# Attention and a gated feed-forward block in one kernel: the late loads and some stores issued by ScalarE's queue, the plan of the order made anew

## The chip, the core and the metric

The kernel runs on one core of one Trainium2 chip. The core has five engines, each with an instruction queue of its own that is worked off in order: TensorE (PE in the profile, with its weight loads as PEld), VectorE (DVE), ScalarE (ACT), GpSimd (POOL) and SyncE (SP). SyncE computes nothing; it issues DMAs. ScalarE can issue DMAs too, and then the issue is one more instruction in the queue that its arithmetic goes through. The metric is the device time of one execution in microseconds, lower is better. Before the change the median of six runs was 271.02 us (270.65 to 273.36).

## The reference, cut to what matters

```python
def _attn_ref(q, k, v, is_retrieval, n_sink, window):     # q, k, v: (4, 8, 768, 64)
    scores = scale * np.matmul(q, k.transpose(0, 1, 3, 2))
    stream_keep = causal & (is_sink | in_win)              # 4 sinks, window of 64
    mask = np.where(retr, full_mask, stream_mask)          # heads 0, 2, 6 see all of the past
    scores = np.where(mask, scores, -1e9)
    a = np.exp(scores - scores.max(-1)); a = a / a.sum(-1)
    return np.matmul(a, v)

def _moe_ref(x, w_gate, w_val, w_out):                     # x: (3072, 512), d_ff = 1536
    g = x @ w_gate
    silu = g * (1.0 / (1.0 + np.exp(-g)))
    return (silu * (x @ w_val)) @ w_out
```

Attention over 4 batches of 8 heads, of which three are causal and five see only 4 sink positions and the last 64; its output, laid out as 3072 tokens of 512, goes through a gated feed-forward block.

## The kernel before, in words

**Tiles.** The 3072 tokens are 24 tiles of 128 queries; two tiles are a pair, and there are 12 pairs, numbered 0 to 11 in the order `QP` (line 142). Six groups of four tiles (`SIZES`, line 149) go through the feed-forward block together. Group 0 is tiles 0 to 3, group 1 tiles 4 to 7, and so on.

**What is done for a pair.** Its q, k and v (called x in the loads) come by one DMA of 512 KB each into a buffer of the ring `raw`, which has 11 buffers (`load`, lines 324 to 340; L330 is q, k and v, L335 and L338 are the weights). The buffers are taken in turn, so that a load can start once the buffer of the load eleven places earlier has been read. Casts (line 185 on DVE and POOL, 183 on ACT) make float16 copies. q and k have to be transposed: for the early pairs by TensorE (`transposes`, L472) with a copy out of PSUM, for the later ones by transposing DMAs (`dmaq` L449 and `dmak` L457, where a `dmak` issues two DMAs). The constants `XQK` and `XK` say from which pair on: 5 for q, 7 for k.

**What is done for a tile.** Scores on TensorE (L594) into PSUM, an exponential on ScalarE (L604, up to 1024 columns at a time), for tiles from 4 on a mask by multiplication on DVE or POOL (L612), the product with v (L624), reciprocal and normalisation (L629, L641). The result `xb` is transposed into `xt`, by TensorE (L657) for tiles below `XBAR` = 8 and by a DMA on SyncE (L651) from there on.

**Feed-forward.** For each group twelve steps j: gate and value products (L875, four matmuls each), tanh on ScalarE (L881), two combinations on DVE (L885, L892); then the output product (L904), copied out of PSUM (`oevac`, on ACT or DVE) and stored by two DMAs of 128 KB (`store`, L928).

**The order.** Every step above is a `Task` with a list of `ways` it can be done (engine and two costs), and the order in which the program is written out is not computed here: it is a string, `ORDER` (line 16). Each two of its digits, in base 62, are a number; below 3700 it is a task, and 3700 + n stands for n matmuls on the identity (`warm`, L305), whose result nobody reads. `WAYS` (line 44) has a digit for each task that picks one of its ways. `Plan.order` (line 102) reads both. So costs, due times and the rings `queue` and `queue2` in the task list leave no trace in the program; what counts is the order of the tasks on each engine and the engine chosen. An engine that reaches a task whose inputs are not there waits, and all that is behind it in its queue waits with it. In the kernel before, all DMAs but one are issued by SyncE: 54 loads, 47 of the 48 halves of stores, and the transposing DMAs (16 for xt, 14 for q, 20 for k).

Of the kernel before, what the change touches and what calls it, by code (L numbers as in the profile page):

```python
# [16 lines left out]
    "000B010A0C0E0D0G0I050F030K2H2I060H04xq07080O2K2J2G0Jy52U090S2L2N2O2Vxv2P2M0L2W022Q0M2z3u2R3t0P2S"  # L17
    "300U322T31yQ2X0T372Y2Z383C0N2a392j0Q1w3D2e2l2k2b3E2m2f0Vxj2n5U2c0c2d1x212p3A2r2o2g2q0R2s3B34330m"
    "xs2u2h3o2v3F3r2t2i0d2w3p0Y2x352y3G0n22xoBM10BWBN1z3H1y3PBO36BX3I0Z3J0o3qBP5VBYBZBQ3K3QBg11Ba28Bq"
    "3L0q3M3sBj3R3b0pBr3T0W3S25Bs3N3U3VBh0r3Oxs3W5R5S0sBi3XxlBt3Y5P5Q23Bu3Z0X3a0u3eBkBR5T3dBb0tBlBSBc"  # L20
    "3c3m0a3f3iBT3hBmBd0vBU240g3n3gBeBn3v3j4dBV3wBoBf0bBv0e3k4PC04cBpBw3l4Q0hC5C1Bx123x4SC2By0fC6C33y"
    "Bz0i27C74X134RC4C80y2B4Y40C90jCA4Z162ACF410z3zCD18CBCG26CC431745444a14CHCK2DCE194B4246CL0kCP4CCM"
    "15CI4b20CQ0w4E2CCR4D0lCeCJ4F1ACU0x2F4H1C29CNCV4I4JCW1BCZ1E4eCO2ECS4GCa4g1D1G4UCTCX4V4WCb4hCf4T4K"
    "1F4i1I4fCYCc47Cd4j1H1K48Cg4k5C4LCh4m4M1J5DCi5ICk4n5E5K1M5J4q5H1L5L4oCl1O4p5G5M4w5FCm4r4xCj1Q4l49"
    "1N6F4zCn4s4y4ACoCq501P5N644t1SCr62675O66521R1UCs53654u6H56Ct4v54Cp1W5557Cw1TCu51614N635Y6q585X1Y"
    "1VCx6s4O6u596v5Z5A6ECy5B1X5W6A6r605b6tD25c7jCzCv6CD3D01ZD75a7PD5D8687R6D7Q5g6B5e5d5h705fD1D4715m"
    "696GD9DC7S7Z5nD6DH7lDD7iDADEDI5o6oDFDJ1a7a6pDB1cDM1bDG7bDKDN7UDPDO1d5iDLDR1eDQ5p7TDS7cDW1g5q1fDT"
    "8VDUDX5j5s8G1i5rDYDb5t1h6yDVDg8H8KDc8U6IDh1jDd5uDZ6JDiDeDa8J6z8I6w6KDl8L8XDqDf6x8Q6L5vDmDjDrDn6M"
    "E0Ds7ODk7kDv966N8R5k976O5wDw8S5l7NDo6PDxDtDp6QDy6RDu1k8T6YDz1mE16Z1l1o5x5y6S8W6a6b6TE26c1n6UE36e"
    "6VE4E66f1p6d6iE76W6j6g5zE86h9h7XE572E96X6k9r737YEC9m6l9k9l7B9jED747C6m9sEE9AA37D7EEA6nEF9i757F76"  # L30
    "EI9tEB98EO9B997HA1EPER7IEQ7V9uET7GESEYEUEG7WA2Am7JEVEZEW7h7K9GEH7fEdEaAn7d8FEXEbEe8EEg7g8O9HEf77"
    "EJEc8M8PEiEh78En8NEjElEk79EoEqEp7L7A95EmEsEr7M1qEx94Et1sEvEy1r1uEu7m9IEzF07nEw1tF2F17oF7F31vFCF8"
    "F47pF9FDEK7q9JFEF5EL7eFMAYEMF67rA0AZFAENAiAc7uAb7sFH7tFBAa80FIAp7vFFAkAj81FJFKAdFG8283FL7w84FN7x"
    "Al7y86858887FO899C7zAo8YFP8A8ZFSFQ9D8B8b8a8CFRFT8c8i9E8DFU8d8j8eFV9FFk8fFWFYFlFX8gFpFm8h9gFuFq9f"
    "FZFrFv8oFwFa8p8kFb8r8qFnFc8sFsFoFd8lFxFt8mFzFyFe8t8nG0G2G1G4G38uG58yFf8v8zG6G78wG8Fg9p8x9KFhG99n"
    "9q9L90GA9MFi9oGC9TGBFjGE9U91AWGJGD92GF9VGOGGGK939WGLGPGiAe9XGQ9ZAXGHAfGM9Y9aAgGIGRGNAh9b9w9xGTGS"
    "9c9zGj9d9NGUGW9O9v9y9eGV9PGY9QGdGXGZ9RGbGaGe9SGfGgGcA4GhH6A5GkH7A6A7GlHBH8A8GmH9HCA9GnGoHAAAGpHD"
    "ABAIACAJGqADHEAKGrHGHFHLHHHJHIGsHMHOHNGtHKHQHPAEHRALAFHVAMHSAGGuHWANAHAOHXHTAPAQHUGvARAqGwArASGx"
    "HaAsGyH0HbATGzAtAUH1AuHcB0AVH2AvB1AwH3HfAxH4HYHgH5AyHdHZAzHhB6B2HeB7HiB3B8HkB4HjB9HlHnB5BAHmBGHp"
    "HoBHBBBCHqI4BDHrHsBEHtI5BFBIHuBJHzBKHvHxHwI0BLI2I1HyISI3IXITIVIUIYIcIZIWIaIdIfIeIbIhIgI6IiIkIjI7"  # L40
    "ImIlI8IrInI9JQIoIsIpItIwIqIuIxIzIyIvJ1J0J6J2JBJ3J7J4J8JCJ9JDJ5JEJAJGJFJLJHJJJIJMJOJNJKJRJPJSJTJW"
    "JUIAJXJVIBJYICJZJcJaIDIGJbIEJdIFIHJeIIJfJiJgIJIMJhIKJjILINJkIOJlJmIPJnIQIR"
)
WAYS = (
    "000010000000000000000000000000000000000000000000000000000000000000000000000000000000000000000000"
    "000000000000000000000000211000010000000010111000010010011000100000000000000000000001000000200010"
    "000000010000000000000000000000011001101000001110110110010000000000100000100000000000000100110000"
    "110000010000000000001001000000000010101001000011001000010010000000000000000000000000100000200000"
    "000100001000000000000000000100000000000010011000000100100000000000000000012000022000000001011010"
    "100010000000000000000000000000100011010000000000110010000000000000001001000000000010001102000000"  # L50
    "000010000000000000000000010110000000000110111001001001000000000010000000000021000210000000001010"
    "001000000000000000000000000000000000000000000000000000000000000000000000000000000000000000000000"
    "000000000000000000000000010000000000010000000000000000000000000000000000000000000000000000000000"
    "000000000000000000010000010000000000000000000000000000000000000000000000000000000000000000000000"
    "000000010000000000000000000000000000000000000000000000000000000000000000000000000000000000000000"
    "000000000000000000000000000000000000000000000000000000000000000000010000000000000000000000000000"
    "0000000000000000000000000000000000000000000000000000000000000000000000000000"
# [55 lines left out]
def kernel(  # L113
# [35 lines left out]
    SIZES = [4, 4, 4, 4, 4, 4]  # L149
# [13 lines left out]
             "h": 2 * NJ, "osb": 2, "gv": 3, "o": 1, "sc": 1, "av": 1, "tr": 1, "queue": 4}  # L163
# [155 lines left out]


# [3 lines left out]
    def load(kind, n):  # L324
        r = buf("raw", [128, 1024], FP, "raw")
        landed[kind, n] = r
        if kind in "qkx":
# [2 lines left out]
            nc.sync.dma_start(  # L330
                out=r.rearrange("p (h x) -> p h x", h=H),
                in_={"q": q, "k": k, "x": v}[kind][b, :, sl, :].rearrange(
                    "h (p j) d -> p h (j d)", j=2))
# [336 lines left out]
    def tasks_of_pair(n):  # L670
# [38 lines left out]
        if xqk:  # L709
            oldq = [x for t in (2 * n - 4, 2 * n - 3) for x in T_sc_of[TILES[t]]]  # L710
            T_dq[n] = [moved(P.add(
                f"dq{n}.{j}", [("SP", 1.27, 1.27, 0)], pos - 0.05,
                (lambda n=n, j=j: dmaq(n, j)), deps=[cs[0, j], T_fill0] + oldq,
                grp=f"pair{n}", takes=["queue", "queue"]), 0.9, 1.1) for j in range(2)]
            T_ev[n, 0] = T_ev[n, 1] = T_dq[n]
        if xk:
            T_ev[n, 2] = [moved(P.add(
                f"dk{n}.{j}", [("SP", 2.5, 2.5, 0)], pos - 0.04,
                (lambda n=n, j=j: dmak(n, j)), deps=[cs[1, j]] + older,
                grp=f"pair{n}", takes=["queue"]), 0.7, 0.7) for j in range(2)]  # L720
# [197 lines left out]

    def store(g, tt):
# [10 lines left out]
    for g in range(NG):  # L930
# [111 lines left out]
```

## Time and profile before

The median is 271.02 us. One execution was profiled; it took 270.79 us, of which 269.0 are the span from its first to its last instruction.

| | |
|---|---|
| median of 6 runs | 271.02 us |
| the profiled execution, its span | 270.79, 269.0 us |
| PE, PEld, DVE busy | 94%, 54%, 61% |
| ACT, POOL busy | 65%, 36% |
| DMA | 42.01 MB, mean 156 GB/s |
| longest chain, by engine | PE 71%, ACT 12%, DMA 7%, SPq 6% |

Busy time of PE counts a matmul until its result is out, and the next one starts long before that, so the start of one to the start of the next is the measure of what a matmul costs. DMA-issuing instructions are not counted as busy time of ScalarE or SyncE; they stand in the order of time with the letter q after the engine's name (SPq, ACTq).

### The profile page before, as it was taken

The numbers are of one execution on the slowest core, as the hardware profiler recorded it, in microseconds if no ns is written. First come the engines' busy times: TensorE is split into PE (matmuls) and PEld (weight loads), VectorE is DVE, ScalarE is ACT, GpSimd is POOL, SyncE is SP. The second block draws the span as 40 slices with busy tenths as digits, with TensorE's granted clock in tenths as the row PEclk, the third lists the DMA queues.
The fourth block names the chain that finished last, engine by engine and source line by source line (L and its number), as shares of the span: only waits on it lengthen the run. The fifth ranks groups of instructions, "written<-read, shape, count | busy, mean of one in ns | idle before, by whom it ended". The sixth has DMA issues, their size and how long they took to land.

```text
span 269.0 us, 5256 instructions
## 1 busy us (share of the span) xinstructions
PE 254.0 (94%) x1971; PEld 146.0 (54%) x1971; DVE 165.0 (61%) x332; ACT 175.9 (65%) x292; POOL 96.8 (36%) x125
## 2 busy tenths in 40 slices
PE   7999789999999999979999899999999999999991
PEld 7877556566655555634446455545555554444440
DVE  7565777688468776458865266677664557775001
ACT  3899998989995996877566654776455643232111
POOL 8748868665293533582065200430021320000000
PEclk9999999999999999999999999999999999999999
DMA  7999999999997977956684811651212200100343
GB/s 192 307 333 331 305 332 379 313 290 288 298 228 187 264 117 200 185 104 140 171 193 75 142 39 22 137 99 23 67 30 62 59 2 20 39 2 0 90 105 78
DMA packets 78520, 42.01 MB, mean 156 GB/s; under 512 B 30880, under 2 KB 73888, under 8 KB 78496
## 3 DMA queue, kind: packets, MB, share of 16 engines
q1 hardware_dynamic: 78416, 41.56, 63.1%
q8 instruction: 15, 0.25, 0.4%
q10 hardware_dynamic: 80, 0.13, 0.2%
q14 instruction: 9, 0.07, 0.1%
HBM read 28.31 MB, written 6.29 MB: 129 GB/s over the span
## 4 chain that ended last, share of the span: by engine, by line
PE 71%; ACT 12%; DMA 7%; SPq 6%; DVE 2%; issue 2%; ACTq 0%
PE gv L875 38%; PE o_ps L904 20%; PE sc L594 7%; PE av L624 4%; DMA raw<-in_v_dram 3%; SPq L330 3%; ACT v L183 3%; ACT e L604 2%; DMA xt<-xb 2%; ACT hq L183 2%; ACT vt L183 2%; ACT sig L881 2%; DMA kT<-hq 1%; SPq L457 1%; DVE sil L885 1%
## 5 line engine op out<-in xcount | busy, mean ns | idle before, releaser
L604 ACT ACTIVATE e<-sc 128x1024 f16<-128x1024 f32 (+4 forms) x71 | 62.3, 881 | 20.6 <-PE sc L594 20.4
L875 PE MATMUL gv<-xt,wg_sb 128*128 128x512 f16 (+1 forms) x304 | 70.3, 368 | 2.9 <-DMA xt<-xb 2.4
L875 PE MATMUL gv<-xt,wv_sb 128*128 128x512 f16 (+1 forms) x304 | 71.0, 368 | 1.1 <-DVE sil L885 1.0
L904 PE MATMUL o_ps<-wo_sb,h 128*128 128x512 f16 x288 | 70.6, 379 | 0.3 <-DVE o_sb L185 0.2
L881 ACT ACTIVATE sig<-gv 128x512 f32<-128x512 f32 (+1 forms) x76 | 43.4, 576 | 41.5 <-PE gv L875 40.4
L885 DVE SCALAR_TENSOR_TENSOR sil<-sig,gv 128x512 f32<-128x512 f32 (+1 forms) x76 | 49.6, 658 | 33.5 <-ACT sig L881 33.0
L612 POOL TENSOR_TENSOR e<-e,m 128x640 f16<-128x640 f16 (+1 forms) x20 | 33.8, 1689 | 60.6 <-ACT e L604 59.0
L892 DVE SCALAR_TENSOR_TENSOR h<-sil,gv 128x512 f16<-128x512 f32 (+1 forms) x76 | 48.6, 655 | 10.3 <-PE gv L875 9.3
L875 PEld LDWEIGHTS <-wg_sb 128*128 128x128 f16 x304 | 28.7, 98 | 30.5 <-issue 2.9
L875 PEld LDWEIGHTS <-wv_sb 128*128 128x128 f16 x304 | 28.9, 98 | 29.9 <-issue 1.9
L904 PEld LDWEIGHTS <-h 128*128 128x128 f16 x288 | 26.9, 98 | 26.0 <-issue 0.7
L594 PE MATMUL sc<-qT,kT 128*128 128x256 f16 (+1 forms) x228 | 35.6, 257 | 1.5 <-ACT e L604 1.5
L594 PEld LDWEIGHTS <-kT 128*128 128x128 f16 x228 | 20.4, 98 | 12.3 <-issue 2.1
L624 PEld LDWEIGHTS <-e 128*128 128x128 f16 x472 | 20.1, 97 | 8.7 <-ACT e L604 1.9
L185 POOL COPY v<-vt 32x528 f16<-32x528 f16 (+1 forms) x34 | 22.1, 651 | 5.6 <-DVE vt L185 4.1
L624 PE MATMUL av<-vt,e 128*128 128x65 f16 x392 | 21.8, 193 | 1.4 <-DVE xb L641 0.8
L185 POOL CAST vt<-raw 64x512 f16<-64x512 f32 x24 | 15.7, 657 | 16.1 <-PE av L624 10.3
L641 DVE TENSOR_TENSOR xb<-av,rc 128x256 f16<-128x256 f32 x47 | 19.9, 424 | 1.6
L183 ACT COPY o_sb<-o_ps 128x512 f32<-128x512 f32 x17 | 9.9, 585 | 14.9 <-PE o_ps L904 13.4
L629 DVE RECIPROCAL rc<-av 128x4 f32<-128x4 f32 x48 | 8.5, 179 | 17.6 <-PE av L624 17.3
L183 ACT COPY v<-vt 2x528 f16<-2x528 f16 (+1 forms) x30 | 18.8, 626 | 0.4
L183 ACT CAST hq<-raw 128x512 f16<-128x512 f32 x27 | 16.2, 617 | 3.7 <-DMA raw<-in_q_dram 2.9
(62 smaller groups left out, 185.5 us busy)
## 6 DMA issues: line engine op xcount, KB each, us to landing
raw<-in_q_dram SPq DMA_DIRECT2D x12, 512.0 KB, 5.3
raw<-in_k_dram SPq DMA_DIRECT2D x12, 512.0 KB, 6.7
raw<-in_v_dram SPq DMA_DIRECT2D x12, 512.0 KB, 6.8
out_dram<-o_sb SPq DMA_DIRECT2D x47, 128.0 KB, 2.4
raw<-in_moe_w_gate_dram SPq DMA_DIRECT2D x6, 512.0 KB, 8.2
raw<-in_moe_w_val_dram SPq DMA_DIRECT2D x6, 512.0 KB, 8.5
raw<-in_moe_w_out_dram SPq DMA_DIRECT2D x6, 512.0 KB, 9.2
kT<-hq SPq DMA_TRANSPOSE x20, 2.4
```

Of the source, the lines that this page charges most:

```text
L183: nc.scalar.copy(out=dst, in_=src)
L185: ENG[task.way[0]].tensor_copy(out=dst, in_=src)
L594: nc.tensor.matmul(sc[c // 4][:, c % 4:c % 4 + n, :], weights, moving, start=first, stop=last)
L604: nc.scalar.activation(out=e[:, 0:n], in_=whole_sc.pop((t, u))[:, 0:n], func=AF.Exp, scale=scale)
L612: ENG[task().way[0]].tensor_tensor(out=ev, in0=ev, in1=mm, op=ALU.mult)
L624: nc.tensor.matmul(av[:, n, 0:65], ee, vv, start=(m == 0), stop=(m == len(bl) - 1))
L641: nc.vector.tensor_tensor(out=xbs[t][:, :, odd, :], in0=av[:, :, 0:64], in1=rc.to_broadcast([128, 4, 64]), op=ALU.mult)
L875: nc.tensor.matmul(ps, wsb[:, kk, j * 128:(j + 1) * 128], xt[:, kk, c[0]:c[1]], start=(kk == 0), stop=(kk == 3))
L881: nc.scalar.activation(out=sg[g, j, c], in_=gs[g, j, c], func=AF.Tanh, scale=0.5)
L885: nc.vector.scalar_tensor_tensor(out=sl[g, j, c], in0=sg.pop((g, j, c)), scalar=1.0, op0=ALU.add, in1=gs.pop((g, j, c)), op1=ALU.mult)
L892: nc.vector.scalar_tensor_tensor(out=hs[g, j][:, c[0]:c[1]], in0=sl.pop((g, j, c)), scalar=0.5, op0=ALU.mult, in1=vs.pop((g, j, c)), op1=A ...
L904: nc.tensor.matmul(o_open[g, tt], hs[g, j][:, tt * 128:(tt + 1) * 128], wo_sb[:, j, :], start=(j == 0), stop=(j == NJ - 1))
```

## The change

Loads of q, k and v for pairs 5 to 11 are issued by ScalarE. A store may be issued by ScalarE too. `XBAR` goes from 8 to 6 and `XK` from 7 to 6. Some costs in the task list are new, and so are the whole of `ORDER` and `WAYS`. In the core of the diff the two strings are cut:

```diff
 ORDER = (
-    "000B010A0C0E0D0G0I050F030K2H2I060H04xq07080O2K2J2G0Jy52U090S2L2N2O2Vxv2P2M0L2W022Q0M2z3u2R3t0P2S"
+    "010B050A000C0E0D0G0I040F062H2I2G0Hxv2P2J2Q0K2K032R0Jxx2U0i2S2V2T2M02xt070L2W2N083txo2X2z2Z0O2Y09"
...
     RINGS = {"raw": 11, "hq": 2, "e": 6, "xb": 3, "xt": 2, "sig": 2, "sil": 3, "ahead": 3,
-             "h": 2 * NJ, "osb": 2, "gv": 3, "o": 1, "sc": 1, "av": 1, "tr": 1, "queue": 4}
+             "h": 2 * NJ, "osb": 2, "gv": 3, "o": 1, "sc": 1, "av": 1, "tr": 1, "queue": 4, "queue2": 3}
...
+    XBAR = 6
+
+    XQK = 5
+    XK = 6
...
         landed[kind, n] = r
+        eng = nc.scalar if late(kind, n) else nc.sync
         if kind in "qkx":
...
-            nc.sync.dma_start(
+            eng.dma_start(
                 out=r.rearrange("p (h x) -> p h x", h=H),
...
+    def late(kind, n):
+
+        return kind in "qkx" and n >= XQK
+
...
-            f"load {kd}{n}", [("SP", 0.6, 1.15, 0)],
+            f"load {kd}{n}", [("ACT" if late(kd, n) else "SP", 0.64, 1.2, 0)],
...
-    XBAR = 8
-
-    XQK = 5
-    XK = 7
...
         for j in range(2):
-            eng = nc.scalar if j and final else nc.sync
+            eng = nc.sync
+            if T_st[g, tt].way[0] == "ACT" or j and final:
+                eng = nc.scalar
             eng.dma_start(out=rows[j], in_=o_sb[j * 64:(j + 1) * 64, :])
...
-            st = P.add(f"st{g}.{tt}", [("SP", 1.16, 1.16, 0)], g + 1 + tt / SIZES[g] + 0.05,
+            st = P.add(f"st{g}.{tt}", [("SP", 1.25, 1.2, 0)] + ([] if final else [("ACT", 1.25, 1.2, 0)]), g + 1 + tt / SIZES[g] + 0.05,
```

Read out task by task, the two orders hold:

| | before | after |
|---|---|---|
| loads issued by SP, by ACT | 54, 0 | 33, 21 |
| stores (two DMAs each) by SP, by ACT | 24, 0 | 15, 9 |
| `xdma` (one transposing DMA each) on SP | 16 | 18 |
| `dk` (two each), `dq` (one each) on SP | 10, 14 | 12, 14 |
| TensorE transposes of `xb` (four matmuls), of q and k (eight) | 8, 12 | 6, 11 |
| `warm` matmuls, the first 40 included | 176 | 137 |

In both, the last half of the store of the last tile is issued by ScalarE. Masks, casts and copies change engine in many places: tasks on ACT 262 and 280 (of these 30 are loads and stores), on DVE 276 and 275, on POOL 88 and 98.

More of the change, by code (lines that the diff above doesn't have):

```diff
@@ L16 @@
 ORDER = (
-    "000B010A0C0E0D0G0I050F030K2H2I060H04xq07080O2K2J2G0Jy52U090S2L2N2O2Vxv2P2M0L2W022Q0M2z3u2R3t0P2S"
[L18 to L41, printed above, removed]
@@ L42 @@
-    "JUIAJXJVIBJYICJZJcJaIDIGJbIEJdIFIHJeIIJfJiJgIJIMJhIKJjILINJkIOJlJmIPJnIQIR"
+    "010B050A000C0E0D0G0I040F062H2I2G0Hxv2P2J2Q0K2K032R0Jxx2U0i2S2V2T2M02xt070L2W2N083txo2X2z2Z0O2Y09"
+    "0j2L30xj2j2a2b2l0M2c2O2e370P2f2d322n2g2k38310U2m39xl2p0N2o3A3C3B2q0S2r2D3D2h3u2u2s2t0V1x3E1w0Q2i"
+    "3sxt3F3q2v0T2w2x3G342y3p0m0RxoBO33BY363H3P3oBZ3I0o0n3JBPBa210q3K3Q3LBQ353Mxv3R0p1y1z3T5U3S3N3UBR"
+    "Bb0W223O0r3bBiBSBc3VBs10Bl3c3r3W0XBj3j3dBk0Y5TBt3kBv113X3l3Y3gBu5R3e3Z0k0Z3f3a5VBwBT3w0lBm3m0cBU"
+    "BW233nBd240dBV3x0a3vBeBXBg255PBfBn3y0sBhC20b3h0uBo3zC7C3Bp0tBqC4C840C9C541280v0gCABr42C60e43Bx44"
@@ new lines @@
+    "CB450h4P4B3i46C0By27124Q47Bz0f4C484X2ECCC14S4d13164c4ECDCF4FCE2B17CH0y4Y4R5S4H5Q4ZCK180zCG4I4a4D"
+    "14CI194b2A4JCJ2C0w154g4eCM4G4h1ACR0xCL20CN4K4jCS26CP1C4kCT1B4L29CO2FCg1E4MCW1G4l1D1I4m4WCQCXCU4V"
+    "1KCY1FCZ5C4i4nCbCV4T1HCh5D5ECa5KCc4oCe4U4p1JCd5F5G4q5LCf4w5H4rCi4x4f1L5M4s60Cj615N5ICmCk1M4y1O4z"
+    "ClCn5O501N49Co5W514A521QCp1P4N53Cs6454Ct4t5J1R68554O5665Cu571S4u666958Cv6H6F1T59CyCw676u5Y625ACz"
+    "1U4v63Cx5Z6C5B6vD06q1V7l6AD45a6sD9Cq6BD5D7D6DACr701W5XDEDB1YD85g1X5bDF5hDCD1DG6p1aDJ6D5c1ZDHDDDK"
@@ new lines @@
+    "6r5e6EDO5f71D2DL5d7T5m1bDPDIDT7R72DQ6G5nDM7SD3DR7U5oDNDU5p1cDVE2731eDSDW1d5q7nDYDX8I7b7k1g5u5r1f"
+    "DbDZ6t5vDd6oDa1h5s8SDeDcDg5t7WDfDi1iDh7cDn1k8K1jDj6yDlDoDk8L8M6IDpDs8T6JDmDq1l8NDtDx8ZDrDu6L6zDy"
+    "5i6KDvDz6w6M5jE0Dw6x8J7d6O6N6S6PE3E11m6Q7QE46T7P7e5k5w6RE51o6Y1n7V5xE87mE6988W6Z6U5lE98U1p6a6bEA"
+    "6c8X6VE7EB6e6W6d8VEE1q6i6f6X5yEF9j1r1s6g6jEG9I6h8Y7499EH5z6k751tEK6l9B9C9n7D6m9mEL9o9J7E6n9lEMEC"
+    "7F7GEQED9k7Z769D7JETER7a7X7H9AESEVAp7KEa7YEUEW77EXEYEb9K787IEfEcEN7L7j7fEZEg7o7MEd8H9L9t8GEh7pEi"
@@ new lines @@
+    "EeAa7qEk1uEpEj9uAkEl79A51vEnEm7i7AEsEqEoA27hFOAlEr8OEuEt8P7B7gEzEvAeF4Ew7C8QAcF0Af7wF1F57rAdEx8R"
+    "AbEOF67s7xF2EPAmEyF796F37u97F9F87v7tFEFAAn9vA3EIFCFB82EJFDFFFJ83FG9w7yFHFK847z7N85A4FLFM86FI7O80"
+    "FPFNAr878A8188FQ9G898BAqFR8C8a9H8DFU8b8EFVAo8F9E8dFW8e9FFm8cFrFnFSFpFoFsFuFtFTFX9h8kFw8lFY9iFqFa"
+    "FxFZFvFzG1Fy8gG2G0G48h8fG68iFbG78jG8Fc8qFd8m8rFg8n8tG3Fh8uG5G98sFe8wGB8vFf8x8o90GAGE8p8yFi8z919M"
+    "9rFj929NGG939s9pGC9O9VGHGDGk9WGF9qGLGI9X9PGJGMFkAZGNGOAYGKFlGQGPGV94GR9QGTGWGS959YGX9RGYAg9Z9S9b"
@@ new lines @@
+    "GUGa9aAh9TGZGfGb9c9UAi9dGc9xA0Gd9eA1GgA6Aj9fGiA7Gl9gGhA9GeH8AA9zHDGj9yA8ACHBH9ADHAGmHCHIHEGnAKHF"
+    "HJABGqALHNAMHGGoAEANAFGpGrAOHKASGsHOAPHLGtGwGuHMATAQGxGvARAGAsAHGyAtHHAIAUHPAvGzHQAJAwH0AVH2AxH1"
+    "AWHSHRHXAuAXHVHYAyHZHTB2H3HUHaHWAzH4B0HcB1HbHhHdHmHeHiHfHjHnB8HoHrHgB9HkHsBAH5BBHpBCHtI6B3BDH6Hl"
+    "BIBEBJHuH7BFHqB4BGB5HwBHB6BKHvHxI1BLB7HyHzBMI2I4I0BNI3I7I5IUI8IXI9IVIZIWICIYIaIAIeIbIBIjIfIcIgIk"
+    "IhIlIdIoIiItIpImIqIuIrIvIwIsIDInIxIyJ3IzJ1J0J4J6J5J2IEJ7J8JDJ9JIJAJEJBJFJJJGJKIFJNJHJCJSJOJLJPIG"
@@ L43 @@
+    "JQJMIHJTJRJUJYJVJZIIJaIJJbJeJcJWIKJdJfJXJgILJkIMJhIOJiINJlJjIPJmIQJnJoIRISJpIT"
 )
 WAYS = (
[L45 to L57, printed above, removed]
+    "000101000000000000000000000000000000000000000000000000000000000000000000000000000000000000000000"
@@ new lines @@
+    "000000000000000000000000100100010000000010010000001010010001100000010000000000000000000002022100"
+    "100000000000000010000000010000000010000001000010011100000000000000100100100000000000000000000110"
+    "000010010000000000001001000000000000000011010001110001100010000000000000000100000000021011000000"
+    "001100000001000000000000100100000000002211101000000000001000000001000000000020111000000000010100"
+    "011000000100000000000001000000002000201200000000101000000100000000000010010000000000001000110000"
@@ new lines @@
+    "000000000000000000000000000102102000000000101000110000000000000000100100000000000000100000000000"
+    "110010000000000000001000000000000000000000000000000000000000000000000000000000000000000000000000"
+    "000000000000000000000100000100000000000000000000000000000000000000000000000000000000000000000000"
+    "000000000100000010000110000000000000000000000000000000000000000000000000000000000000000000000100"
+    "000100000010000100000000000000000000000000000000000000000000000000000000000000000110000010000000"
@@ L58 @@
+    "000010000000000000000000000000000000000000000000000000000000000000000100000000000010000010000000"
+    "000000000000000000000000000000000000000000000000000000000000000010000100000000"
 )
@@ L357, in moved @@
                      deps=[issue], grp=issue.grp)
-        if "queue" in issue.takes:
-            P.uses(issue, "queue", done)
+        for r in ("queue", "queue2"):
+            if r in issue.takes:
+                P.uses(issue, r, done)
         return done
@@ L368 @@
             after=[T_dma, T_seq.get("load") if kd in "qkx" else None],
-            takes=["raw", "queue"], grp=f"L{n if kd in 'qkx' else kd}")
+            takes=["raw", "queue2" if late(kd, n) else "queue"], grp=f"L{n if kd in 'qkx' else kd}")
         T_load[kd, n] = moved(T_iss[kd, n], d + (0.6 if at == 0 else 0), 0.75 if at < 5 else 2.0)
@@ L711, in tasks_of_pair @@
             T_dq[n] = [moved(P.add(
-                f"dq{n}.{j}", [("SP", 1.27, 1.27, 0)], pos - 0.05,
+                f"dq{n}.{j}", [("SP", 1.37, 1.33, 0)], pos - 0.05,
                 (lambda n=n, j=j: dmaq(n, j)), deps=[cs[0, j], T_fill0] + oldq,
@@ L717, in tasks_of_pair @@
             T_ev[n, 2] = [moved(P.add(
-                f"dk{n}.{j}", [("SP", 2.5, 2.5, 0)], pos - 0.04,
+                f"dk{n}.{j}", [("SP", 2.62, 2.56, 0)], pos - 0.04,
                 (lambda n=n, j=j: dmak(n, j)), deps=[cs[1, j]] + older,
@@ L856, in tasks_of_tile @@
             xt = P.add(
-                f"xdma{t}", [("SP", 1.25, 1.25, 0)], pos + 0.08, (lambda t=t: xtranspose(t)),
+                f"xdma{t}", [("SP", 1.33, 1.29, 0)], pos + 0.08, (lambda t=t: xtranspose(t)),
                 deps=norms, takes=takes + ["queue"], grp=f"tile{t}", after=[lead])
@@ L917, in oevac @@
             copy(T_oe[g, tt], o_sb, o_ps)
+    T_st = {}
     def store(g, tt):
@@ L998 @@
             P.uses(head, ring, oe)
+            T_st[g, tt] = st
             P.uses(oe, "osb", moved(st, 0.6, 1.2))
```

## The prediction

> **What bounds the kernel now.** First the page's sums and its chain of waits:
>
> ```profile
> span 269.0 us, 5256 instructions
> ...
> PE 254.0 (94%) x1971; PEld 146.0 (54%) x1971; DVE 165.0 (61%) x332; ACT 175.9 (65%) x292; POOL 96.8 (36%) x125
> ...
> PE 71%; ACT 12%; DMA 7%; SPq 6%; DVE 2%; issue 2%; ACTq 0%
> ```
>
> TensorE bounds, but 254.0 us counts matmuls whose time overlaps. From start to start in the timeline a 512-column matmul costs 0.216 us, 256 columns 0.109, a transpose or 128 columns 0.056, a product with v 0.0295. With the counts of the groups by form (835, 270, 216 without the warm ones, 472, and two of 384 columns at 0.16) this is 180.4 + 29.4 + 12.1 + 13.9 + 0.3 = 236.1 us of needed work. The other 32.9 us are what a change of order can win: 1.4 ahead of the first matmul, 9.9 for 176 warm matmuls, 5.8 from the last one to the end of the span, and 15.8 of waiting. The second view, the busy time by stretch (PE, PEld, DVE, ACT, POOL; clock, DMA share, GB/s), says where:
>
> ```profile
> 20.00:30.00 10.00, 8.71 (x108) 7.08 (x108) 5.92 (x18) 9.80 (x18) 8.87 (x13) 1.00 1.14 323
> 30.00:40.00 10.00, 8.15 (x67) 5.48 (x65) 7.40 (x17) 9.82 (x22) 6.56 (x10) 1.00 1.09 321
> ...
> 60.00:70.00 10.00, 9.34 (x99) 6.11 (x98) 6.59 (x15) 9.83 (x16) 3.59 (x5) 1.00 1.05 289
> 70.00:80.00 10.00, 9.49 (x93) 5.91 (x92) 6.38 (x15) 9.87 (x18) 7.32 (x11) 1.00 1.19 268
> ...
> 110.00:120.00 10.00, 8.43 (x60) 4.31 (x57) 5.22 (x11) 7.98 (x12) 8.19 (x10) 1.00 0.73 105
> ...
> 150.00:160.00 10.00, 9.00 (x66) 4.91 (x64) 4.05 (x8) 6.67 (x12) 0.89 (x1) 1.00 0.40 85
> ```
>
> Three stages. Up to 40 us the DMA is full (share above 1) and so is ScalarE: start-up. From 60 to 80 us ScalarE works 9.8 of 10 us and TensorE idles 1.2 us. From 100 to 160 us ScalarE has room and TensorE idles 3.0 us (all stretches together), at two places worst of all. The chain in order of time names who is late there:
>
> ```profile
> 113.83 2.43 DMA xt<-xb
> 116.39 1.02 PE gv L875 x4
> ...
> 130.21 1.36 SPq L330
> 131.61 0.58 SPq L330
> 132.24 2.76 SPq L457
> 135.04 3.41 DMA kT<-hq
> ...
> 149.02 2.55 DMA xt<-xb
> 151.71 1.02 PE gv L875 x4
> ```
>
> Before groups 2 and 3 TensorE waits for a transposing DMA, and around 130 us k's transposes stand behind loads in SyncE's queue. SyncE's timeline between 60 and 136 us is unbroken but for 0.05 us between DMAs and four waits, three of 0.5 us and one of 0.2. This is its issue time when its own queue was short, then with a third load close behind:
>
> ```profile
> 60.69 0.58 SPq L330 DMA_DIRECT2D raw<-in_q_dram  x1
> 61.37 0.65 SPq L330 DMA_DIRECT2D raw<-in_k_dram  x1
> 62.06 1.58 SPq L330 DMA_DIRECT2D raw<-in_v_dram  x1
> ```
>
> **The change, part by part.**
>
> **Work taken from TensorE.** Two `xtr` of four and one `tr` of eight matmuls go: 16 x 0.056 = -0.9 us. They lie in the stage where TensorE sets the end or waits for ScalarE, so nearly all counts. The copies behind them (two of 0.42 us, one of 1.03) go too; the one on ScalarE is in the count below.
>
> **SyncE.** 21 loads (0.62 us with the gap) and nine stores (1.22 for two DMAs) leave, two `xdma` and four transposes of `dk` (1.3 each) come: 13.0 + 11.0 - 7.8 = 16.2 us less. Counted up to the first gate product of group 2, at 116.4 us, it has 51 loads, 6 stores, 6 `dk`, 5 `dq`, 4 `xdma` = 66.3 us in the old order and 33, 5, 7, 4, 6 = 57.9 in the new. Eight us of slack are more than any wait of that stage. What is late next is the normalisation on DVE that every `xdma` waits for, and the landing itself, 2.4 us. Of the 3.0 us of idle time by stretch (4.6 us if counted from start to start) I take -3.0; bounds 0 and -4.6. The two new `xdma` come ahead of group 1's first gate; before, the four transposes and the copy took under 1 us there and now it is 1.2 + 2.4, hidden while group 0's output products are left for TensorE, and up to 2.5 us late if not, which I count with the upper ends below.
>
> **ScalarE up to group 1.** Its work ahead of the first gate product of group 1 (74.9 us), counted off both orders with start-to-start durations:
>
> | us each | kind | before | after |
> |---|---|---|---|
> | 0.92 | 1024 columns | 19 | 18 |
> | 0.49 | 512 columns (exp, tanh, copies) | 24 | 22 |
> | 0.52 | casts of q, k | 18 | 17 |
> | 0.61 | casts of v, spread q | 12 | 10 |
> | 1.27, 1.30 | copies of sink and band rows | 4, 4 | 3, 4 |
> | | small ones, in all | 7.8 us | 9.4 us |
> | 0.62 | issues of loads | 0 | 8 |
>
> The sums are 63.9 and 65.6 us. ScalarE before was 11.0 us behind its own work there (74.9 - 63.9: its start and its idle time), and full, so it set the time. TensorE's needed work ahead of that point is 52.8 and 52.4 us. With 11.0 kept, the new order gets there at 76.6, 24.2 us behind TensorE's work instead of 22.0: +2.1 us. The stores on ScalarE come after 90 us of TensorE's needed work; 9 x 1.22 = 11.0 us are hidden, as ScalarE is busy for 5 to 8 of 10 us from 100 to 220 us. Uncovered they would cost up to 11.0.
>
> **What an issue costs on ScalarE.** The trace has one, the last half store: `263.95 0.55 ACTq L928`, with nothing else being issued. The other end is SyncE's own price for the same eight loads, 2.13, 1.68, 1.59, 0.58, 0.65, 1.58, 0.59, 0.84 = 9.6 us, against 5.0 in the table: +4.7. Waits on semaphores stand as gaps in SyncE's row, so these durations are the queue being full. The pattern is that two loads go in at 0.6 and the third is held. ScalarE's queue starts empty and the new order spaces its loads; only x5 comes close behind two others. So 0.62 each and 1.0 for x5: +1.0, bounds 0 and +4.7. Behind a held issue stand exponentials and tanh, and TensorE waits for these. A load also waits for the buffer of eleven loads back: q5, k5, x5, k6 and q7 for weight casts on POOL, which has 4 to 6 us more to do up to there. On SyncE that wait delayed loads only.
>
> The Trainium skill (Perfetto Trace Analysis, DMA Instruction — HWDGE) speaks against the change: one descriptor generator is shared by the two sequencers and locked by the one that issues. In this trace the ScalarE issue starts 0.26 us after SyncE's last one ended, so no run here shows a wait for the lock. By that rule eight issues beside a SyncE that is busy with 1.25 us transposes or held loads would each wait some 0.5 us, an estimate, 4 us in all, and the sum below would be +1.2 instead of -1.8.
>
> **Start-up.** 39 warm matmuls fewer are 2.2 us by 0.056. They fill waits for data, so only data that come earlier make it a gain. The first scores have 4.5 us of ScalarE's work ahead of them instead of 6.6; but DMAs are full either way, k1 and x1 are the fifth and eighth load in both orders, and a weight of the last steps (g5) now comes sixth. As ScalarE sets the time at 75 us, a faster start helps only by what it cuts from ScalarE's idle time, 2.9 us between 10 and 60 us. I take -1.0; bounds -2.2 and +1.0 (POOL late with casts).
>
> **The end.** The last store is issued by ScalarE after its last copy, two issues, as SyncE did: 0.47 and 0.59 then, 0.55 each now: 0.
>
> **Sum** against the profiled execution: -0.9 - 3.0 + 2.1 + 1.0 - 1.0 = -1.8; a span of 267.2 and 269.0 us in all instead of 270.79. The median, 271.02, is 0.23 above that execution, so the forecast is **269.2 us**.
>
> **The rivals.**
>
> *ScalarE is held by its loads* (slower). Its eight issues cost what they cost SyncE, +4.7 instead of +1.0: the sum is +1.9, 272.9 us. For it: DMA share above 1 from 10 to 80 us, and no reserve on ScalarE there. Against it: an own queue, and gaps between the loads. It decides from 2.8 us over the eight loads, 0.35 us each.
>
> *SyncE's relief is worth nothing*: TensorE waits before groups 2 and 3 for normalisation, not for a queue, or the new plan spends the slack. The 3.0 us stay: +1.2, 272.2 us. For it: `113.83 2.43 DMA xt<-xb` was issued right after its copy and normalisation. Against it: the chain at 130 us runs through SyncE's loads.
>
> *All of it comes off*: every wait after 100 us (-4.6), the full start-up (-2.2), no held issue: -0.9 - 4.6 + 2.1 - 2.2 = -5.6, 265.4 us. For it: fewer warm matmuls planned. Against it: DMAs that are full.
>
> That the change doesn't do what it says is no rival here: loads and engine are in the code.
>
> **How the numbers follow.** Forecast 0.44, ScalarE held 0.28, relief worth nothing 0.11, all of it 0.17. A measurement can tell 0.5%, 1.36 us, from no change. The forecast's own range is 267.2 to 271.0; 0.35 of its 0.44 lie beyond 0.5%, 0.09 within. Relief worth nothing gives 0.08 within, 0.03 slower. So faster 0.35 + 0.17 = 0.52, same 0.17, slower 0.31. Both rivals at the ends are to be held, with 1 us beyond the slower one, whose price is the least known: 265.2 to 273.9.
>
> **What would show it.** Right: the stretches from 100 to 160 us with under 1.6 us of TensorE's idle time; `ACTq` issues of 0.5 to 0.65 us between 50 and 110 us, but for one or two; the first gate of group 1 at 74 to 77 us; SyncE with gaps. Wrong: `ACTq` rows of 1.5 us and more with exponentials behind them, or that gate later than 78 us (ScalarE held); TensorE's idle time unchanged before groups 2 and 3 (relief worth nothing); that gate ahead of 73 us (the start-up was worth more than I took).

## The result, and the profile after

The changed kernel takes 274.30 us (median of 36 runs, 272.64 to 278.79) against 271.38 us for the kernel before in the same sessions (73 runs): the ratio is 1.0092, 95% interval 1.0073 to 1.0112. It is slower by 0.9%. The ratio leaves out executions more than 1.5% above the fastest of their kernel, so it is not the quotient of the two medians (1.0108). The forecast was 269.2 us. The profiled execution has a span of 273.2 us instead of 269.0; it took 275.07 us, 0.8 more than the median.

The page's sums and its longest chain, after the change:

```profile
span 273.2 us, 5134 instructions
...
PE 251.8 (92%) x1916; PEld 143.2 (52%) x1916; DVE 165.7 (61%) x326; ACT 168.8 (62%) x283; POOL 102.7 (38%) x143
...
PE 62%; ACT 12%; DMA 12%; DVE 7%; issue 2%; ACTq 1%; SPq 1%; POOL 0%; POOLq 0%; DVEq 0%
```

TensorE has less to do and waits more: its share of the chain fell from 71% to 62%, that of DMAs rose from 7% to 12%. SyncE's issues fell from 6% to 1%, so that queue was indeed relieved. Counted as in the prediction, needed work went from 236.1 to 235.2 us and the first and last idle stretches changed little; what grew is waiting. The busy time by stretch (columns as before) says where:

```profile
20.00:30.00 10.00, 7.54 (x95) 6.18 (x96) 5.19 (x15) 9.59 (x23) 8.83 (x16) 1.00 1.09 310
30.00:40.00 10.00, 8.85 (x73) 5.83 (x71) 7.07 (x15) 8.36 (x16) 7.75 (x7) 1.00 1.06 314
...
60.00:70.00 10.00, 9.42 (x88) 5.81 (x89) 6.85 (x13) 8.16 (x15) 4.16 (x7) 1.00 0.89 240
70.00:80.00 10.00, 7.11 (x66) 3.79 (x63) 3.44 (x7) 7.79 (x13) 3.83 (x6) 1.00 1.03 243
...
110.00:120.00 10.00, 7.28 (x70) 4.30 (x67) 3.10 (x9) 5.09 (x8) 0.13 (x1) 1.00 1.01 208
...
150.00:160.00 10.00, 9.96 (x70) 5.24 (x69) 4.92 (x10) 5.93 (x11) 2.12 (x1) 1.00 0.51 105
```

From 70 to 80 us TensorE now idles 2.9 us instead of 0.5, and ScalarE, which was full there, works 7.8 of 10 us: it is no longer the one that is late. From 110 to 120 us the idle time rose from 1.6 to 2.7 us, while from 150 to 160 us the wait of 1.0 us is gone. The chain of waits names the two places (start, duration, what):

```profile
72.99 0.42 DVE xb L648
73.42 0.88 DVE hq L185 x2
74.30 5.09 DMA xt<-xb
79.39 0.05 issue
79.43 3.63 PE gv L882 x16
...
111.81 6.14 DMA kT<-hq
...
118.62 0.43 DVE xb L648
...
119.10 0.76 PE av L631 x20
```

Tile 7 is normalised at 73.4 us (`xb`; the two casts `hq` that the chain puts behind it are other work). Its transposing DMA, one of the two that the change adds, is issued at 74.3 us and lands 5.1 us later; group 1's first gate product starts with it, at 79.4 us instead of 74.9. At 111.8 us a transpose of k takes 6.1 us to land, and a normalisation on VectorE comes only after it. The timeline shows what stood in the queues:

```profile
52.09 0.59 ACTq L337 DMA_DIRECT2D raw<-in_k_dram  x1
...
54.45 3.54 ACTq L337 DMA_DIRECT2D raw<-in_v_dram  x1
...
58.04 0.62 ACT L183 CAST hq<-raw 128x512 f16<-128x512 f32 x1 [2.99 <-issue]
...
58.71 0.40 PE L479 MATMUL tr<-ident,hq 128*128 128x128 f16 x4 [0.41 <-ACT hq L183]
...
70.18 1.34 SPq L456 DMA_TRANSPOSE qT<-hqz  x1
70.26 0.38 ACTq L337 DMA_DIRECT2D raw<-in_q_dram  x1
...
73.01 1.20 SPq L939 DMA_DIRECT2D out_dram<-o_sb  x2
...
74.30 1.32 SPq L658 DMA_TRANSPOSE xt<-xb  x1
...
118.07 0.43 DVE L185 CAST hq<-raw 128x512 f16<-128x512 f32 x1 [5.10 <-DMA kT<-hq]
```

One load, x5, the third in a row, held ScalarE for 3.54 us; the cast behind it came late and TensorE waited for that cast. In the trace x5's issue waits for no semaphore, and SyncE issued nothing from 53.1 to 64.6 us, so neither a buffer nor SyncE's issues held it. The other 20 loads cost ScalarE 0.37 to 0.72 us each, also beside a transpose that SyncE issued at the same time (70.2 us). Tile 7's transpose stood behind a store until 74.2 us. And a cast at 118.07 us waited 5.1 us at the head of VectorE's queue for a buffer, with a normalisation behind it that TensorE needed.

Summed from matmul start to matmul start, the waits of TensorE that are new in this execution are 1.69 us at 47 us (two), 1.77 at 58 (two), 2.99 at 76 and 2.64 at 116 us; gone are 1.89 before group 2 (two), 0.60 at 140 and 1.16 before group 3. By stretch, waits and warm matmuls took 1.3 us less up to 45 us, then 3.7 more up to 65, 2.1 more up to 85, 1.4 more from 105 to 130 and 1.8 less from 130 to 165 us.

### The profile page after: what moved, and what is told of

Its sections match the earlier page's. It is cut to its first block, busy times and chain, and to the rows that moved or that the text cites. A ratio compares the mean times of both kernels' runs of the same rounds, so it can differ in the third digit from the quotient of the medians.

```text
span 273.2 us, 5134 instructions
## 1 busy us (share of the span) xinstructions
PE 251.8 (92%) x1916; PEld 143.2 (52%) x1916; DVE 165.7 (61%) x326; ACT 168.8 (62%) x283; POOL 102.7 (38%) x143
## 4 chain that ended last, share of the span: by engine, by line
PE 62%; ACT 12%; DMA 12%; DVE 7%; issue 2%; ACTq 1%; SPq 1%; POOL 0%; POOLq 0%; DVEq 0%
PE gv L882 32%; PE o_ps L911 18%; PE sc L601 5%; DMA kT<-hq 4%; DMA raw<-in_q_dram 4%; PE av L631 4%; ACT e L611 4%; PE warm L305 2%; ACT sig L888 2%; DVE sil L892 2%; DMA xt<-xb 2%; ACT v L183 2%; ACT hq L183 2%; DMA raw<-in_k_dram 2%; ACTq L337 1%
## 5 line engine op out<-in xcount | busy, mean ns | idle before, releaser
L619 POOL TENSOR_TENSOR e<-e,m 128x1024 f16<-128x1024 f16 (+1 forms) x16 | 28.9, 1809 | 76.0 <-ACT e L611 69.6
L185 POOL COPY v<-vt 2x528 f16<-2x528 f16 (+1 forms) x40 | 25.7, 643 | 7.4 <-ACT vt L183 4.6
L185 POOL CAST vt<-raw 64x512 f16<-64x512 f32 x27 | 17.3, 641 | 21.3 <-issue 13.5
L648 DVE TENSOR_TENSOR xb<-av,rc 128x256 f16<-128x256 f32 x45 | 19.1, 424 | 1.6
L183 ACT CAST hq<-raw 128x512 f16<-128x512 f32 x24 | 14.7, 623 | 8.3 <-issue 3.0
L619 DVE TENSOR_TENSOR e<-e,m 128x1024 f16<-128x1024 f16 (+1 forms) x22 | 15.0, 688 | 5.8 <-ACT e L611 5.8
L183 ACT COPY v<-vt 32x528 f16<-32x528 f16 (+1 forms) x24 | 15.1, 628 | 0.4
```

Source lines behind the costliest of these rows:

```text
L183: nc.scalar.copy(out=dst, in_=src)
L185: ENG[task.way[0]].tensor_copy(out=dst, in_=src)
L619: ENG[task().way[0]].tensor_tensor(out=ev, in0=ev, in1=mm, op=ALU.mult)
L648: nc.vector.tensor_tensor(out=xbs[t][:, :, odd, :], in0=av[:, :, 0:64], in1=rc.to_broadcast([128, 4, 64]), op=ALU.mult)
```

## The experiments

Here *before* and *after* are the old and the changed kernel. The theory: the loss comes from waits that the new order and the two new tile transposes made, above all the landing of tile 7's transpose. The rivals: ScalarE is held by the loads it issues; or two queues that move data at once make transposes land late, whatever the order.

### Which engine issues

```diff
-        return kind in "qkx" and n >= XQK
+        return False
...
-            if T_st[g, tt].way[0] == "ACT" or j and final:
+            if j and final:
```

> The order of after, but the 21 late loads and the nine stores are issued by SyncE again, at the same places of the order. Theory (order): the 3.3 us lost against before are waits that the new order and the two new tile transposes made, at 58, 76 and 116 us; which engine issues a load hardly matters, so the time stays at 273 to 276 us: the gaps at 58 us (x5 held on ScalarE, 1.8 us) go, but SyncE again has 16 us more to issue and the transposes land later. Rival 1 (ScalarE is held by its issues): the loads cost ScalarE about 14 us in all, back on SyncE the time falls to 271 us or below. Rival 2 (two queues): transposing DMAs land late because loads of another queue share the 16 DMA engines with them; with one queue kT lands 2.4 us after its issue again between 80 and 125 us, not 4.7, and group 1's first gate comes ahead of 78 us instead of 79.4.

277.51 us, ratio to before 1.0223 (1.0187 to 1.0260). So moving the issues to ScalarE is worth 3.2 us in the new order; rival 1 falls. TensorE's new waits here are 1.71 us at 87, 1.29 at 117 and 3.14 us at 122 us, the last for a transposing DMA before group 2. x5's 1.77 us at 58 us are gone, 1.18 us at 73 us came. Rival 2 got its landing at group 1, though not its time (chain of waits):

```profile
74.79 2.77 DMA xt<-xb
77.55 0.05 issue
77.60 1.92 PE gv L882 x8
```

With no second queue, tile 7's transpose landed after 2.8 us instead of 5.1; TensorE was out of other work sooner and still waited 2.51 us for it. Between 80 and 125 us the median landing of k's transposes was 3.7 us, against 4.8 in after and the 2.4 expected: half right.

Only the first of the two edits:

> After with the 21 late loads issued by SyncE again, the nine stores still by ScalarE. With loads and stores both back the time was 277.5 us, 3.2 more than after. Theory (what SyncE is relieved of matters where its queue is full, up to 125 us; the ScalarE stores come later, where it has gaps): this one takes 276.5 to 278 us, the loads are all of the 3.2. Rival (the stores are half of the issue time, so half of the relief): 275 to 276 us.

278.30 us, ratio 1.0253 (1.0218 to 1.0289). The intervals of the two overlap: the loads are all of the effect, the stores on ScalarE bring nothing that can be told.

### Tiles 6 and 7 on TensorE again

```diff
-    XBAR = 6
+    XBAR = 8
```

In the order, each transpose stands where TensorE has just done scores or an output product, its copy on VectorE close behind.

> After with XBAR at 8 again: tiles 6 and 7 are transposed by TensorE (0.22 us each) and copied by VectorE; all else as in after. Theory (the landing of tile 7's transposing DMA sets group 1's start): the wait of 2.99 us ahead of group 1's first gate is gone, the gate starts at 76.3 to 77.3 us instead of 79.4, and the time falls by 1.5 to 2.7 us, to 271.6 to 272.8 us. Rival (ScalarE is late by its loads and casts and would hold group 1 anyway): the gate moves by less than 1 us, or ScalarE's exponentials hold TensorE by 2 us more within the next 20 us, and the time stays within 0.7 us of after's 274.3.

271.17 us, ratio 0.9985 (0.9957 to 1.0012): 3.1 us less than after, a little more than expected, and level with before. The gate starts at 76.2 us. The stretch from 75 to 80 us, first of after, then of this kernel:

```profile
75.00:80.00 5.00, 2.13 (x16) 0.97 (x15) 0.69 (x1) 3.09 (x5) 0.44 (x1) 1.00 1.23 289
```

```profile
75.00:80.00 5.00, 4.79 (x29) 2.30 (x27) 2.65 (x5) 3.83 (x7) 0.84 (x3) 1.00 0.97 268
```

TensorE works 4.8 of 5 us instead of 2.1. With tile 7 alone on TensorE:

```diff
-        if t >= XBAR:
+        if t >= XBAR and t != 7:
...
-        if t < XBAR:
+        if t < XBAR or t == 7:
```

> After with only tile 7 transposed by TensorE, tile 6 by a DMA as in after. Theory (only the last tile of the group has no time left for its landing): tile 6's DMA, issued at 71.6 us, lands by 77 us at the latest, so the gate comes at 76.2 to 77.2 us and the time is that of tiles 6 and 7 together, 270.8 to 272.0 us. Rival (two tiles' landings, both late): the gate at 77.5 to 78.5, time 272.3 to 273.5 us.

272.11 us, ratio 0.9998 (0.9960 to 1.0036), the gate at 75.8 us. The median lies 0.1 us above what was expected, the intervals of the two overlap, and the gate is as early: the last tile of the group is the one that matters.

### The same edit in the kernel before

```diff
-    XBAR = 8
+    XBAR = 6
```

> Before with XBAR at 6, the same order and no other change: the two transposes that went from TensorE to SyncE, alone. Theory (the failed step of the prediction is the landing of tile 7's transpose ahead of group 1): in the old order SyncE is late with its loads there, so the transpose is issued late and lands in the same queue; group 1's first gate comes 2.5 to 6 us later than 74.9 us, and the time rises by 1.5 to 5 us over before. Rival (the wait needs the second queue beside it; alone the two transposes are hidden by group 0's output products, as the prediction took them): the gate moves by less than 1 us and the time stays within 0.7 us of before.

278.27 us, ratio 1.0250 (1.0221 to 1.0280). Without a second queue, with the old order, the two transposes cost 6.9 us. The chain of waits, then SyncE's timeline:

```profile
74.13 5.32 DMA xt<-xb
79.44 0.05 issue
79.49 1.89 PE gv L875 x4
```

```profile
73.50 0.53 SPq L330 DMA_DIRECT2D raw<-in_q_dram  x1
74.13 1.29 SPq L651 DMA_TRANSPOSE xt<-xb  x1
```

The gate comes 4.6 us late. The landing is as long as in after, here with a load of 512 KB issued just ahead in the same queue. That the time rose above the expected 5 us has a second part: the four matmuls at 79.49 us took 1.89 us, 0.43 from start to start instead of 0.216. The granted clock is half from 78.0 to 84.8 us, and the matmuls that ran in that time lost 2.6 us; see the last section.

### When the loads beside tile 7 are issued

```diff
-ACT load q7 (70.3 us), load k7 (72.7 us)
 ACT ex8.0
+ACT load q7, load k7
```

> After with the issues of pair 7's q and k (ScalarE, at 70.3 and 72.7 us) moved behind the first exponential of tile 8 in ScalarE's queue (about 76 us), nothing else; xt of tiles 6 and 7 still goes by transposing DMAs. Theory (the loads of the second queue share the DMA engines with tile 7's transpose): it lands 2.5 to 3.5 us after its issue instead of 5.0, group 1's first gate comes at 76.5 to 78.0 us, and the time falls by 1 to 2.5 us from 274.3. Rival (the landing is long because of what SyncE's own queue holds, or of the load of pair 6's v that is under way in any case): it lands after 4.5 us or more and the time stays within 0.7 us.

277.28 us, ratio 1.0220 (1.0184 to 1.0257): worse, against both expectations. Without the two issues ScalarE reached the exponential earlier than I had reckoned, and the loads went out together with the transpose. Timeline, then chain:

```profile
73.41 1.42 SPq L658 DMA_TRANSPOSE xt<-xb  x1
73.53 0.40 ACTq L337 DMA_DIRECT2D raw<-in_q_dram  x1
73.97 0.76 ACTq L337 DMA_DIRECT2D raw<-in_k_dram  x1
```

```profile
73.41 7.01 DMA xt<-xb
```

The landing took 7.0 us. A miss for the place, but a third point on the line. The fourth, with both behind the first tanh of group 1:

```diff
-ACT load q7 (70.3 us), load k7 (72.7 us)
 ACT tanh1.0.0
+ACT load q7, load k7
```

> After with the issues of pair 7's q and k moved behind the first tanh of group 1 in ScalarE's queue, nothing else. In the earlier move they were reached at 73.5 us, at the same time as tile 7's transposing DMA (73.4), and it then landed after 7.0 us, against 5.0 in after and 2.8 with all loads on SyncE. Theory (loads under way on the second queue delay the landing): now no load is issued from 68 us to the gate, the transpose lands 2.4 to 3.3 us after its issue, the gate comes at 76.2 to 77.7 us, and the time is 271.5 to 273.2 us. Rival (the landing depends on SyncE's own queue, the load move was an accident): 4.5 us and more, time 274 and above.

The view of the tile xt between 70 and 80 us, then ScalarE's DMA issues and a combination on VectorE in the timeline:

```profile
DMA to landing us min/median/max: 2.4/2.5/2.5
```

```profile
77.64 0.37 ACTq L337 DMA_DIRECT2D raw<-in_q_dram  x1
...
78.06 0.91 ACTq L337 DMA_DIRECT2D raw<-in_k_dram  x1
...
79.04 1.01 ACTq L337 DMA_DIRECT2D raw<-in_v_dram  x1
...
80.09 2.25 ACTq L337 DMA_DIRECT2D raw<-in_q_dram  x1
...
82.50 2.08 ACTq L337 DMA_DIRECT2D raw<-in_k_dram  x1
...
83.07 0.69 DVE L892 SCALAR_TENSOR_TENSOR sil<-sig,gv 128x512 f32<-128x512 f32 x1 [1.60 <-ACT sig L888]
```

Tile 7's landing is 2.4 us, the gate at 76.6 us and its wait 0.26 us, as the theory has it. The time is not: 275.16 us, ratio 1.0108 (1.0072 to 1.0145), no less than after. Five loads now came within 5 us, ScalarE was held by the later ones, and TensorE waited 1.28 us at 82, 1.02 at 84 and 1.66 at 95 us for tanh, exponentials and what follows. Here the prediction's rival, ScalarE held by its loads, is real; in the order of after it is x5 alone.

### The held load and the cast in front

```diff
-ACT load x5
 ACT cq4.0, ex6.2, cq4.1, ck4.0
+ACT load x5
```

> After with the issue of pair 5's v moved behind the casts of pair 4's q and k in ScalarE's queue, nothing else. Theory: the issue was held 3.54 us because it was the third in a row; behind the casts it costs 0.4 to 0.8 us, the two waits of TensorE at 57.9 and 58.9 us (1.77 us together) go to under 0.4 us, and group 1's first gate comes 0 to 1.8 us earlier, less than 1.8 where tile 7's DMA lands no earlier. Time down by 0.5 to 1.8 us. Rival (the wait for group 1 is set elsewhere and swallows it): the gap at 76 us grows by as much as the two at 58 us shrink, and the time stays within 0.4 us. Rival 2 (the issue is held wherever it stands, since the DMA engines are full): 2 us and more again.

274.77 us, ratio 1.0116 (1.0083 to 1.0149): no gain. The issue cost 0.38 us and both waits at 58 us are gone, but the wait for tile 7 grew from 2.99 to 3.57 us, and seven of the matmuls behind it ran at half speed. The time is close to rival 1's (0.5 us from after, where it said 0.4), though the wait took back only 0.6 of the 1.8 us and the slow matmuls lost 1.7 more. The hold differs between executions of the same instructions: 3.54 us in after, 3.11 with tiles 6 and 7 on TensorE, 1.88 in the next kernel; in two others the second load of the three was held too, for 1.25 and 1.58 us.

```diff
-DVE ck10.0
 DVE nm11.1, oe1.2, nm11.0
+DVE ck10.0
```

> After with one cast (first half of pair 10's k, on VectorE, whose buffer waits for a transposing DMA of pair 8) moved behind the two normalisations of tile 11, nothing else. Theory: this cast stood 5.1 us at the head of VectorE's queue with the normalisation behind it, and the wait of 2.64 us at 116 us goes to under 0.3 us; part of it comes back ahead of group 2's first gate, because tile 11's transposing DMA is issued by SyncE behind pair 9's k and lands at 121 to 122.5 us while the gate could start at 120.5; so the time falls by 0.7 to 2.2 us. Rival (the normalisation is not what is late; TensorE's clock of waits there is set by ScalarE or by the landing): all of it comes back within 10 us and the time stays within 0.4 us.

274.43 us, ratio 1.0102 (1.0067 to 1.0138). The wait at 116 us is gone; 1.17 us came ahead of group 2's gate. The time did not move, which is the rival's figure, but this execution too lost time behind the wait for tile 7, as the granted clock (third column from the right) shows:

```profile
75.00:80.00 5.00, 2.38 (x6) 0.87 (x7) 0.27 (x1) 1.96 (x4) 0.74 (x2) 0.77 0.98 253
80.00:85.00 5.00, 5.00 (x32) 2.50 (x31) 3.73 (x8) 2.68 (x5) 0.00 (x0) 0.89 0.46 133
```

What the cast alone is worth stays open.

### Toward a faster version

```diff
+XBAR = 8 and tile 11 on TensorE
+ACT load x5 behind ck4.0
+DVE ck10.0 behind the copy of tile 11
```

> After with four edits together: tiles 6 and 7, and 11 as the last of group 2, are transposed by TensorE; pair 5's v is issued behind the casts of pair 4; the cast of pair 10's k stands behind tile 11's normalisations. Theory: with tiles 6 and 7 alone it was 271.2 us, with waits left of 1.19 us at 58.7 (held issue) and 1.22 at 118.5 us (tile 11's DMA); these two go, less 0.22 us for TensorE's transposes and what comes back, so 269 to 270.3 us, faster than before by 0.4 to 0.8%. Rival (ScalarE sets the pace up to group 1, so that a wait removed at 58 us comes back by 76): 270.3 to 271.2 us.

270.33 us, ratio 0.9963 (0.9936 to 0.9990): ahead of before by a hair, at the border of theory and rival. The gates of groups 1 and 2 start at 74.2 and 117.2 us.

```diff
+PE sc6.0 behind gate0.8.0
+ACT load q11, load k11 behind tanh2.0.0
+ACT ck10.1 behind tanh2.1.0
```

> The version with tiles 6, 7 and 11 on TensorE, x5 later and the cast of pair 10's k later (270.3 us), with three more moves: the scores of tile 6's first unit behind a gate product of group 0 (they wait 1.05 us for a copy at 47.5 us), the second half of pair 10's k cast and the loads of pair 11's q and k behind the first tanh of group 2. Theory: 0.6 us ahead of group 2 (loads under way delay the landing of tile 9's and 10's transposes) and 0.8 us behind it (tanh behind a cast that waits for a buffer) go, and 0 to 0.9 us at 47.5 us: 268.1 to 269.2 us. Rival (ScalarE and VectorE set the pace there): 269.7 to 270.5 us.

272.20 us, ratio 1.0010 (0.9974 to 1.0045). Both missed. The second moved load waited in ScalarE's queue until a transpose of q had landed (issued at 114.5 us, 6.2 us), the exponential and the second tanh of group 2 stood behind it (3.17 us), and TensorE waited 2.44 us for what that tanh feeds (timeline):

```profile
120.75 0.38 ACTq L337 DMA_DIRECT2D raw<-in_k_dram  x1
121.18 1.02 ACT L611 ACTIVATE e<-sc 128x1024 f16<-128x1024 f32 x1 [3.17 <-DMA qT<-hqz]
```

Why that load waits for that transpose is not shown.

The old kernel with the last tiles of groups 2 and 3 on TensorE:

```diff
-        if t >= XBAR:
+        if t >= XBAR and t not in (11, 15):
...
-        if t < XBAR:
+        if t < XBAR or t in (11, 15):
```

> Before with the last tiles of groups 2 and 3 (tiles 11 and 15) transposed by TensorE instead of by DMA, the same order, all loads and stores on SyncE. Theory (before groups 2 and 3 it is the landing of the last tile's transpose that is late, and taking it off SyncE needs no second queue): the waits of 1.51 and 1.16 us ahead of the two gates go, 0.45 us of transposes come, so the time falls by 1.5 to 2.5 us to 268.9 to 269.9 us. Rival (the prediction's: SyncE is behind with its issues, so that other DMAs of the two groups land as late): the waits shrink by less than half, the time stays above 270.4 us.

269.18 us, ratio 0.9900 (0.9864 to 0.9935), a span of 267.6 us: the fastest of all, with loads and stores on SyncE. Its stretches:

```profile
110.00:120.00 10.00, 9.57 (x78) 5.21 (x75) 6.37 (x15) 8.69 (x14) 8.76 (x11) 1.00 0.84 124
...
150.00:160.00 10.00, 10.00 (x70) 5.32 (x69) 5.48 (x10) 6.46 (x12) 0.28 (x1) 1.00 0.34 74
```

TensorE idles 0.4 us where it idled 1.6, and none where it idled 1.0. Eight matmuls do what 21 loads on another engine were to do.

## Why the prediction was wrong, point by point

The sum was -1.8 us on the span; measured is +4.2 in the profiled executions (+2.9 by the medians). Two terms, of 3.0 and 2.7 us, make nearly all of the 6.0 us between them: group 1's first gate came 4.5 us later than before where the terms ahead of it gave 1.2, and from there to the end the new order won 0.3 us where 3.0 were taken.

- **The step that failed** is the sentence on the two new `xdma`: "1.2 + 2.4, hidden while group 0's output products are left for TensorE", taken as nothing in the sum. The last of the products left started at 76.2 us, the transpose was issued at 74.3, behind a store, and landed after 5.1 us: 2.99 us of waiting. Taking tile 7 off the DMA again gave 3.1 us back, and putting tiles 6 and 7 on it in the old kernel cost 6.9 us. The 2.4 us came from rows with no load close ahead; with loads close ahead tile 7's landing was 5 to 7 us. The bound of 2.5 us was named, but not put into the sum. With tiles 6 and 7 off the DMA the new order still takes 271.2 us, 2.0 above the forecast; that is the next term.
- **SyncE's relief**, -3.0: idle time of TensorE from 100 to 160 us was 3.0 us before and is 2.8 after. The relief itself is real: the waits at 140 and 150 us are gone, and the same order without it is 3.2 us slower. But the wait before group 2 was replaced, by 2.64 us at 116 us, a normalisation behind a cast behind a buffer behind a transpose. That the new order spends the slack was the second rival, and its time is 272.2 us. What spends it is shown only in part: with that wait taken out the time did not fall (274.43 us; 1.17 us came back at the gate, and the profiled execution lost clock behind tile 7's wait). Two transposed tiles on TensorE take the gate waits off without any relief.
- **ScalarE up to group 1**, +2.1 and a gate at 74 to 77 us: borne out, once tile 7 is out of the way (75.8 and 76.2 us; all terms ahead of the gate together give 76.1). The two waits at 47 us, for copies on VectorE and ScalarE, belong to it; its 2.1 us were not measured apart. In the changed kernel the gate came at 79.4 us, which the prediction's last paragraph would have read as ScalarE held; its 7.8 us of 10 say otherwise.
- **Issues on ScalarE**, +1.0 with x5 alone held: 20 of 21 at 0.37 to 0.72 us, and x5 alone held, as said. x5 was mis-sized: 1.77 us of waiting where 1.0 was taken. The rival of all eight held did not come about, though its 272.9 us lies nearest to the time measured.
- **The rule on the descriptor generator**: the page (the Trainium skill, Perfetto Trace Analysis, DMA Instruction — HWDGE) names VectorE and SyncE, and a note under it says that which two engines issue is a choice of the compiler and the mechanism the same. The changed kernel shows no such wait: nine loads that ScalarE issued while SyncE was in the midst of issuing a transpose (1.2 to 1.8 us) took 0.37 to 0.45 us, where 0.5 us of waiting each had been estimated.
- **TensorE's work**, -0.9, and **start-up**, -1.0: 0.9 us and, as waits and warm matmuls up to 45 us, 1.3 us were found. The waits from 45 to 85 us, 5.8 us more than before, swallowed both.

One reading in the prediction was wrong. It gave the second rival that the transpose at 113.83 us was issued right after its normalisation. A tile is normalised in two halves; the 24th half, the last that group 2 needs, was ready at 110.9 us, and two transposes of k stood ahead in SyncE's queue (timeline of the kernel before):

```profile
110.47 0.42 DVE L641 TENSOR_TENSOR xb<-av,rc 128x256 f16<-128x256 f32 x1
110.67 3.06 SPq L457 DMA_TRANSPOSE kT<-hq  x2
113.83 1.22 SPq L651 DMA_TRANSPOSE xt<-xb  x1
```

So SyncE's queue was late there, as the forecast had it. In the changed kernel the same transpose is issued at 120.59 us, its normalisation having ended at 120.56: the queue is no longer what is late, the normalisation is.

## What to carry to other kernels

A transpose moved from TensorE to a DMA trades 0.2 us of a busy engine for a landing, and the landing must be priced with the loads that are in flight at that moment; where the consumer comes next, as for the last tile of a group, keep it on TensorE. Moving issues to another queue relieves the old one, but a queue of arithmetic can be held by the third load in a row, and a transpose then lands late beside loads that it no longer stands behind. Take the waits from the profile one at a time, and look for the cheapest edit to each, before a plan is made anew.

## What the runs showed of the hardware

Tile 7's transpose landed 2.4 us after its issue with no load issued in the 6.9 us before it, 2.8 with one at 3.6 us before on the same queue, 5.1 with loads on the second queue at 1.6 and 4.0 us before, 5.3 with one 0.6 us before on the same queue, and 7.0 with two issued at the same moment on the second. The Trainium skill (DMA: Bandwidth & Descriptors, Queues, rings and completion order) says that each engine goes round the queues that have work, a packet at a time; the 7.0 us fit that, and the 5.3 us show that one queue alone makes it as long.

A long wait can cost twice. Behind seven of eleven waits of TensorE of 2.4 us and more, the profile shows half the granted clock for 3.41 us (once 6.83): 512-column matmuls ran at 0.43 us instead of 0.216, five to ten of them, and with the narrower ones 1.5 to 2.6 us were lost; behind waits of 2.51, 2.64, 2.99 and 3.14 us in other profiles none did. The Trainium skill (TensorE: Matmul & The Clock Gate, What's actually happening) says that the clock halves after an idle window of about 3.4 us that runs freely. Here waits of 2.44 to 2.85 us sufficed in some executions, so the figure is no lower bound for a wait; two profiles have half the clock for 3.41 us at 31 us, where no wait of the ten us before was above 1.3 us. The changed kernel's times, 272.6 to 278.8 us, go with the mean granted clock in part: nine executions at 0.993 to 0.995 took 272.6 to 273.7 us and six at 0.980 to 0.982 took 275.2 to 275.9, but the profiled one, at 0.998, took 275.07.
